# Two chunks' products in four quarters of PSUM's rows, three places for w, test scratch in PSUM, and a planned ScalarE in the first chunks

## Chip, cores and metric

One Trainium2 chip, one core. The metric is the device time of one execution in microseconds (us), smaller is better. Engines: TensorE (PE in the profile, PEld its weight loads), VectorE (DVE), ScalarE (ACT), GpSimd (POOL), and SyncE (SP), whose queue issues nearly all DMAs.

## The reference

A recurrent attention over 4 x 8 heads, 768 positions and head size 40, followed by two feed-forward layers ("MoE") on all 3072 tokens of width 320. Float32 throughout.

```python
state = zeros((B, H, 40, 40))
for t in range(768):
    y[:, :, t] = einsum('bhd,bhde->bhe', r_t, state)
    Sa = einsum('bhde,bhe->bhd', state, a_t)
    state = state * w_t[:, :, None, :] - einsum('bhd,bhe->bhde', Sa, b_t)
    state = state + einsum('bhd,bhe->bhde', v_t, k_t)
x = y as (3072, 320)
x = maximum(maximum(x @ w1, x @ w2), x @ w3) @ w_out        # d_ff 768
h = x @ w_in                                                # d_ff 2048
out = (h * tanh(log1p(exp(h)))) @ w_out2
```

## The kernel before

**Attention.** The 768 positions go in chunks of 32 (C), the 32 heads in two groups of 16, so 48 chunks follow each other, c = 0 to 47. Two chunks make a unit n (24 units). What depends on no state is done ahead of the chain: `pre(n)` takes the running product of w (the scan, L238), its reciprocal by Ln and Exp with a Newton step (L242 to L256), a test of that by Square (L258), scales a (GpSimd, L250), k and b (VectorE, L261 and L265), and multiplies them (L274). Four units make a batch, and `solve(k)` inverts their triangular systems in 31 steps on VectorE (L306, L308). `chain(c)` is the sequence by which chunk c needs the state that chunk c - 1 left: x0 (L382), u (L396), u transposed (L407, L410) and copied beside r (L413), the products of r by u and v (`products`, L349), a triangular mask on them (L418), y and the new state (L430 to L437).

**The products.** `products(h, g)` multiplies r of chunk h by u of chunk h, and r of chunk g = h + 1 by v of chunk g, ahead of time. For each of 16 heads it is a matmul of 40 rows, 32 weight columns and 32 moving columns, which TensorE's records show as two records each. Its output goes to one bank of PSUM, tile `cg`, 128 rows x 512 columns: rows 64 (c % 2) for v, rows 32 further for u, columns 32 ho for head ho. So one call writes two of the four quarters of 32 rows, for u the one half, for v the other.

**Slots.** `run` gives each chunk five slots. In a slot come in turn a step of `chain`, filler (`fill`), a step of the units in `advance`, steps of the solve, and the next step of `chain`. The filler is, in chunks 0 to 5, the conversion of the first MoE's weights (24 blocks), two steps of the pipeline in a slot, a new block every two steps; from chunk LAG = 6 the first MoE's groups of tokens, whose units of 8 matmuls fill TensorE between the steps of the chain, and from chunk 37 on the second MoE's weights beside them.

**The weights' conversion.** The weights come as float64 words. `from64` loads a block (`raw`, 4 places), tests its range (Square, Exp, each with an accumulated sum that the test wants; the element results, written to `t`, are not used), then makes float32 of the two words: ScalarE turns the low word (L580), VectorE shifts and merges the high one into `t` (L581, L582), GpSimd adds (L584). `put` splits it into high and low parts (ScalarE L593, GpSimd L599, VectorE L638).

**w.** `load_w(n)` loads a unit's w to a tile with one place (units 1 to 3 of the start go elsewhere); w is read by the scan and its tile is then scratch up to the Square L258. The load of the next unit's w is traced right behind that Square.

**Order.** The program is built with a planner that places instructions by a model of their times. Inside `tc.manual_schedule(engines=...)` the named engines keep the order of the program: TensorE and VectorE always in attention, ScalarE too. GpSimd and SP take the planner's order. Each engine works off its own queue in order.

## Time and profile before

| | |
|---|---|
| time, median of 3 (lowest to highest) | 1113.77 us (1111.48 to 1116.03) |
| profiled execution: time, span of its instructions | 1112.2 us, 1110.4 us |
| mean granted TensorE clock, share of full speed | 0.99 |
| busy: TensorE, VectorE, ScalarE, GpSimd | 944.8, 864.0, 729.4, 339.0 us |

Times in the rows are us from the start of the span, durations of one instruction are ns where the row says mean. "A <- B" after a row's idle time is what ended that idle time.

### The profile page before, as it was taken

Reading aid. Unit: us, or ns where it says so; the run is one execution under the profiler, and the core shown is the slowest. Engines: PE = TensorE matmul, PEld = TensorE weight load, DVE = VectorE, ACT = ScalarE, POOL = GpSimd, SP = SyncE. Lnnn points to the kernel's source line nnn. Section 1 sums busy time; section 2 is a strip of 40 time slices with the busy share of each in tenths; the row PEclk is TensorE's granted clock in tenths of the full one; section 3 lists DMA queues with packets and bytes.
Section 4 is the critical chain, followed back from the end, with each engine's and each line's share of the span. In section 5 each row is a group of like instructions: output and inputs, shape, how many; then the busy total and the mean of one; then the engine's idle time right before and its main releaser. Section 6 shows DMA issues by size and latency. Waiting matters only on the chain.

```text
span 1110.4 us, 34043 instructions
## 1 busy us (share of the span) xinstructions
PE 944.8 (85%) x14098; PEld 848.1 (76%) x14098; DVE 864.0 (78%) x1650; ACT 729.4 (66%) x1886; POOL 339.0 (31%) x422
## 2 busy tenths in 40 slices
PE   1333435699999999999998999988999999999996
PEld 1222324588888888898897888987899898899896
DVE  7767778968867876876677565879898989888885
ACT  4445775365655665555556777657888787878875
POOL 8436676132322433232113333664020202020000
PEclk9999999999999999999998999998999999999998
DMA  9224442234344343433424443431010101010000
GB/s 244 84 70 118 110 140 49 69 88 110 92 105 106 85 124 75 112 102 79 101 51 120 110 125 106 134 114 43 2 52 1 53 1 53 1 53 1 25 1 27
DMA packets 110614, 87.02 MB, mean 78 GB/s; under 512 B 72740, under 2 KB 89764, under 8 KB 110452
## 3 DMA queue, kind: packets, MB, share of 16 engines
q1 hardware_dynamic: 109712, 84.54, 28.1%
q8 instruction: 113, 1.85, 0.7%
q14 instruction: 49, 0.40, 0.1%
q10 hardware_dynamic: 740, 0.23, 0.1%
HBM read 72.16 MB, written 12.58 MB: 76 GB/s over the span
## 4 chain that ended last, share of the span: by engine, by line
PE 64%; DVE 15%; ACT 10%; issue 3%; DMA 3%; POOL 2%; SPq 0%; ACTq 0%; DVEq 0%; POOLq 0%
PE bps L648 5%; PE cops L976 5%; PE cops L974 5%; PE cops L975 5%; PE cgps L349 4%; PE ys L430 4%; PE bps L798 4%; PE cps L649 4%; PE cps L648 4%; PE cps L650 4%; PE bps L649 4%; PE bps L650 3%; DVE T L308 2%; DVE tv L306 2%; ACT ls L327 2%
## 5 line engine op out<-in xcount | busy, mean ns | idle before, releaser
L648 PE MATMUL bps<-bxh,bw 128*128 128x256 f32 x432 | 139.8, 324 | 9.6 <-ACT mx L755 7.2
L649 PE MATMUL bps<-bxl,bw 128*128 128x256 f32 x432 | 123.8, 287 | 4.2 <-DVE bxl L661 4.2
L650 PE MATMUL bps<-bxh,bw 128*128 128x256 f32 x432 | 122.6, 284 | 0.0
L760 POOL TENSOR_TENSOR hl<-mx,hh 128x256 fp32r<-128x256 f32 x72 | 58.0, 806 | 172.1 <-ACT hh L759 165.1
L648 PEld LDWEIGHTS bps<-bxh,bw 128*128 128x128 f32 x432 | 82.3, 190 | 23.9 <-ACT mx L755 14.5
L250 POOL TENSOR_TENSOR ax<-ax,pp 40x256 f32<-40x256 f32 x96 | 76.7, 817 | 45.6 <-DMA ax<-in_A_dram 16.5
L649 PEld LDWEIGHTS bps<-bxl,bw 128*128 128x128 f32 x432 | 82.9, 192 | 6.7 <-DVE bxl L661 6.5
L308 DVE TENSOR_TENSOR T<-T,tv 128x31 f32<-128x31 f32 (+15 forms) x186 | 81.9, 441 | 6.4
L430 PE MATMUL ys<-rs,ls 128*40 128x72 f32 x1536 | 65.2, 244 | 23.0 <-issue 10.7
L650 PEld LDWEIGHTS bps<-bxh,bw 128*128 128x128 f32 x432 | 82.6, 191 | 0.0
L958 ACT ACTIVATE e<-e 128x512 f32<-128x512 f32 x93 | 58.5, 629 | 34.9 <-DVE e L956 34.4
L286 POOL TENSOR_SCALAR_AFFINE_SELECT ax<-akT 32x256 f32<-32x256 f32 x96 | 48.6, 506 | 107.0 <-DVE akT L281 103.0
L962 DVE SCALAR_TENSOR_TENSOR e<-e,r 128x512 f32<-128x512 f32 x93 | 74.6, 802 | 7.2 <-ACT r L960 7.1
L385 ACT COPY X<-x0ps 128x160 f32<-128x160 f32 x48 | 14.0, 291 | 100.5 <-PE x0ps L382 100.4
L430 PEld LDWEIGHTS ys<-rs,ls 128*40 128x40 f32 x1536 | 56.7, 128 | 29.1 <-issue 12.0
L274 PE MATMUL m<-bk,ax 40*32 40x64 f32 x1536 | 44.2, 261 | 40.7 <-DVE bk L265 21.4
L970 DVE TENSOR_TENSOR gl<-e,gh 128x512 fp32r<-128x512 f32 x93 | 64.6, 695 | 16.3 <-ACT gh L969 15.6
L798 PE MATMUL bps<-hh,bo 128*128 128x256 f32 x360 | 76.2, 294 | 1.3 <-ACT hh L759 1.3
L757 DVE TENSOR_TENSOR mx<-bps,mx 128x256 f32<-128x256 f32 x144 | 60.4, 420 | 20.1 <-PE bps L652 9.8
L418 DVE TENSOR_TENSOR rs<-cgps,cst 64x512 f32<-64x512 f32 x48 | 33.1, 689 | 50.8 <-PE cgps L349 50.4
L274 PEld LDWEIGHTS m<-bk,ax 40*32 40x32 f32 x1536 | 33.6, 132 | 49.0 <-POOL ax L250 29.9
L349 PE MATMUL cgps<-rs,uT 40*32 40x32 f32 x1536 | 64.7, 201 | 7.1 <-ACT uT L410 5.1
(210 smaller groups left out, 3239.6 us busy)
## 6 DMA issues: line engine op xcount, KB each, us to landing
bk<-in_KB_dram SPq DMA_DIRECT2D x24, 448.0 KB
sv<-in_SV_dram SPq DMA_DIRECT2D x96, 80.0 KB
raw<-in_w_dram SPq DMA_DIRECT2D x18, 384.0 KB
w<-in_W_dram SPq DMA_DIRECT2D x21, 231.0 KB
v<-in_VT_dram SPq DMA_DIRECT2D x48, 96.0 KB
rs<-in_RT_dram SPq DMA_DIRECT2D x48, 96.0 KB
cxl<-x SPq DMA_DIRECT2D x12, 384.0 KB
raw<-in_wo_dram SPq DMA_DIRECT2D x13, 320.0 KB
```

Of the source, the lines that this page charges most:

```text
L250: nc.gpsimd.tensor_tensor(out=xv[:, h], in0=xv[:, h], in1=P[ro, h, 0:C], op=ALU.mult)
L274: nc.tensor.matmul(out=ps[32 * zo:32 * zo + 32, cc, jj], lhsT=x[ro, y, 4 * g + jj, cc], rhs=bk[ro, 4 * g + jj, 64 * cc:64 * cc + 64], star ...
L308: nc.vector.tensor_tensor(out=T[:, s + 1:C, 0:s + 1], in0=T[:, s + 1:C, 0:s + 1], in1=tv, op=ALU.subtract)
L349: self.nc.tensor.matmul(out=self.cg[row:row + 32, C * ho:C * ho + C], lhsT=x[0:40, ho], rhs=self.rs[c % 2][0:40, 0:4, ho], start=True, sto ...
L430: nc.tensor.matmul(out=self.ys[64 * y:64 * y + 40, p, 0:72], lhsT=l[:, y, p], rhs=r_[:, :, 4 * (p % 4) + 2 * (1 - y) + p // 4], start=True ...
L648: nc.tensor.matmul(out=ps, lhsT=h[:, k], rhs=xh[:, k], start=(k == 0), stop=False)
L649: nc.tensor.matmul(out=ps, lhsT=h[:, k], rhs=xl[:, k], start=False, stop=False)
L650: nc.tensor.matmul(out=ps, lhsT=l[:, k], rhs=xh[:, k], start=False, stop=False)
L757: after(1, lambda ps=ps, mx=mx: nc.vector.tensor_tensor(out=mx, in0=ps, in1=mx, op=ALU.max))
L798: nc.tensor.matmul(out=pss[d][rows], lhsT=lhsT, rhs=rhs, start=first, stop=last)
L962: nc.vector.scalar_tensor_tensor(out=e, in0=e, scalar=1.0, in1=r, op0=ALU.add, op1=ALU.mult)
L970: nc.vector.tensor_tensor(out=gl, in0=e, in1=gh.bitcast(F32), op=ALU.subtract)
```

## The change

- `products` runs over 8 column places and two halves of the heads: head 8 hi + k of both chunks goes to rows 64 hi (v) and 64 hi + 32 (u), columns 256 (c % 2) + 32 k. One call now writes all four quarters of the rows in turn. The mask is applied in two instructions of 64 x 256 in place of one of 64 x 512.
- w gets a pool of three places, and its load is traced two units ahead, at the head of `pre`.
- In the first MoE's weights the Square and Exp of the range test write to a scratch tile in PSUM (one place), and a block has one more pipeline step between load and test.
- `run` becomes a generator that stops once, before chunk LAG. Up to there ScalarE is not among the engines in program order; from there it is.

```diff
--- before.py
+++ after.py
@@ -162,6 +162,7 @@
         const = pool("a_const", 1)
         pers = pool("a_pers", 1)
         self.p1 = pool("a_1", 1)
+        self.pw = pool("a_w", 3)
         self.ps_m1 = pool("ps_m1", 1, space=PSUM)
         self.ps_kb = pool("ps_kb", 1, space=PSUM)
         self.ps_sm = pool("ps_sm", 1, space=PSUM)
@@ -214,7 +215,7 @@
             t = self.T if n == 2 else self.tr[n // 2]
             self.w[n] = t.rearrange("p t i -> p (t i)")[0:112, 0:528]
         else:
-            self.w[n] = self.p1.tile([128, 528], F32, name="w", tag="w")[0:112]
+            self.w[n] = self.pw.tile([128, 528], F32, name="w", tag="w")[0:112]
         self.nc.sync.dma_start(out=self.w[n], in_=self.A["W"][n // NU, n % NU])
 
     def load_a(self, n):
@@ -232,6 +233,8 @@
 
     def pre(self, n):
         nc, p1 = self.nc, self.p1
+        if NB <= n + 2 < 2 * NU:
+            self.load_w(n + 2)
         x, bk, P = self.ax[n % self.NX], self.bk[n % self.NK], self.pp[n % self.NP][0:R]
         w = self.w.pop(n)
         Pv = P[:, :, 1:33]
@@ -259,8 +262,6 @@
         bv = bk[0:R].rearrange("r p (c s t) -> r (p c) s t", c=2, s=2)
         Qv = Q.unsqueeze(2).to_broadcast([R, 16, 2, C])
         nc.vector.tensor_tensor(out=bv[:, 0:8], in0=bv[:, 0:8], in1=Qv[:, 0:8], op=ALU.mult)
-        if NB - 1 <= n < 2 * NU - 1:
-            self.load_w(n + 1)
         yield
         nc.vector.tensor_tensor(out=bv[:, 8:16], in0=bv[:, 8:16], in1=Qv[:, 8:16], op=ALU.mult)
         if n >= NB:
@@ -342,12 +343,14 @@
 
     def products(self, h, g):
 
-        for ho in range(16):
-            for c, x, row in ((h, self.uT, 32), (g, self.v, 0)):
-                if c is not None:
-                    row += 64 * (c % 2)
-                    self.nc.tensor.matmul(out=self.cg[row:row + 32, C * ho:C * ho + C], lhsT=x[0:40, ho],
-                                          rhs=self.rs[c % 2][0:40, 0:4, ho], start=True, stop=True)
+        for k in range(8):
+            for hi in range(2):
+                for c, x, row in ((h, self.uT, 32), (g, self.v, 0)):
+                    if c is not None:
+                        row += 64 * hi
+                        col = 256 * (c % 2) + C * k
+                        self.nc.tensor.matmul(out=self.cg[row:row + 32, col:col + C], lhsT=x[0:40, 8 * hi + k],
+                                              rhs=self.rs[c % 2][0:40, 0:4, 8 * hi + k], start=True, stop=True)
 
     ZZ = [(jj, zo, 1 - zo // 2, zo % 2) for jj in range(4) for zo in (0, 2, 1, 3)]
 
@@ -415,10 +418,12 @@
         yield
 
         self.products(c, c + 1 if c + 1 < 2 * NCH else None)
-        nc.vector.tensor_tensor(
-            out=r_[64:128, 0:4], in0=self.cg[64 * i:64 * i + 64].rearrange("p (h b i) -> p b h i", b=4, i=8),
-            in1=self.mask[64:128].rearrange("p (b i) -> p b i", b=4).unsqueeze(2).to_broadcast([64, 4, 16, 8]),
-            op=ALU.mult)
+        for hi in range(2):
+            nc.vector.tensor_tensor(
+                out=r_[64:128, 0:4, 8 * hi:8 * hi + 8],
+                in0=self.cg[64 * hi:64 * hi + 64, 256 * i:256 * i + 256].rearrange("p (h b i) -> p b h i", b=4, i=8),
+                in1=self.mask[64:128].rearrange("p (b i) -> p b i", b=4).unsqueeze(2).to_broadcast([64, 4, 8, 8]),
+                op=ALU.mult)
         yield
         yield
 
@@ -515,6 +520,8 @@
         for c in range(NC):
             n, cc = divmod(c, 2)
             chain = self.chain(c)
+            if c == LAG:
+                yield
             for slot in range(5):
                 if slot == 0 and cc == 0 and self.place[n] == 0 and k == self.batch[n]:
                     finish(solve)
@@ -561,18 +568,19 @@
     return stage
 
 
-def from64(nc, stage, src, n, cols, gate, put, beside=False):
+def from64(nc, stage, src, n, cols, gate, put, beside=False, junk=None):
 
     raw, t = stage(n, cols)
     nc.sync.dma_start(out=raw, in_=src.bitcast(I32).rearrange("p k (f w) -> p k f w", w=2))
-    yield
-    yield
+    for _ in range(3 if junk else 2):
+        yield
     low, high = raw[:, :, :, 0], raw[:, :, :, 1]
     tf = t.bitcast(F32)
-
-
-    nc.scalar.activation(out=tf, in_=high.bitcast(F32), func=AF.Square, accum_out=gate.le(2.0 ** 33))
-    nc.scalar.activation(out=tf, in_=tf, func=AF.Exp, scale=-(2.0 ** 20), accum_out=gate.le(0.25))
+    q = junk.tile([128, n, cols], F32, name="junk", tag="junk") if junk else tf
+
+
+    nc.scalar.activation(out=q, in_=high.bitcast(F32), func=AF.Square, accum_out=gate.le(2.0 ** 33))
+    nc.scalar.activation(out=q, in_=q, func=AF.Exp, scale=-(2.0 ** 20), accum_out=gate.le(0.25))
     yield
     if beside:
         nc.vector.tensor_scalar(out=low, in0=low.bitcast(mybir.dt.uint32), scalar1=2.0 ** -29, scalar2=None, op0=ALU.mult)
@@ -628,7 +636,7 @@
         return (x[:, 0:256].rearrange("p (k f) -> p k f", k=2), x[:, 256:512].rearrange("p (k f) -> p k f", k=2),
                 x[:, 512:640])
 
-    def load(self, j, stage, beside=False, pool=False):
+    def load(self, j, stage, beside=False, pool=False, junk=None):
         nc = self.nc
         h, l, m = self.parts(j)
 
@@ -637,7 +645,7 @@
             yield from split_to(nc, h, l, t[:, 0:2], pool)
             nc.vector.tensor_tensor(out=m[64:128], in0=t[64:128, 2], in1=m[64:128].bitcast(F32), op=ALU.subtract)
 
-        return from64(nc, stage, self.src[j], 3, 128, self.gate, put, beside)
+        return from64(nc, stage, self.src[j], 3, 128, self.gate, put, beside, junk)
 
     def mm(self, ps, j, x):
 
@@ -674,6 +682,7 @@
         wp = pool("b_w", 1)
         self.stage = ExitStack()
         self.tmp = staged(pool("b_t", 4, ctx=self.stage))
+        self.junk = pool("b_j", 1, ctx=self.stage, space=PSUM)
         ws = [wp.tile([128, 6, 640], F32R, name="b" + n) for n in ("w1", "w2", "w3")]
         self.w = [Weights(self.nc, A[n], [w[:, j] for j in range(6)], gate) for n, w in zip(("w1", "w2", "w3"), ws)]
 
@@ -695,9 +704,9 @@
     def weights(self):
         for j in range(6):
             for w in self.w:
-                yield w.load(j, self.tmp)
+                yield w.load(j, self.tmp, junk=self.junk)
         for j in range(6):
-            yield from64(self.nc, self.tmp, self.A["wo"][j], 1, DM, self.gate, lambda t, j=j: self.put_out(t[:, 0], j))
+            yield from64(self.nc, self.tmp, self.A["wo"][j], 1, DM, self.gate, lambda t, j=j: self.put_out(t[:, 0], j), junk=self.junk)
 
     def put_out(self, t, j):
         nc, o = self.nc, self.o[:, j]
@@ -831,7 +840,7 @@
         for j, (_, tag, i) in enumerate(low + [(0, "ab0", i) for i in range(3)]):
             self.spots[1, j] = keep, tag, i
         self.raws = [(keep, raw), (keep, "ab0")]
-        self.ts = [(att.p1, "w"), (att.p1, "Q"), (att.const, "rst")]
+        self.ts = [(att.pw, "w"), (att.p1, "Q"), (att.const, "rst")]
         self.loaded, self.running = set(), []
 
     def beside(self, c):
@@ -1203,8 +1212,11 @@
                     if c >= EARLY:
                         moe2.beside(c)
 
+                chunks = att.run(fill)
+                with tc.manual_schedule(engines=IN_ORDER):
+                    next(chunks)
                 with tc.manual_schedule(engines=IN_ORDER | {mybir.EngineType.Activation}):
-                    att.run(fill)
+                    finish(chunks)
                     moe2.jobs = []
                     while moe2.running:
                         moe2.beside(0)
```

## Rows read from the trace of the kernel before

**Rows 1.** The page: the span, the busy time of each engine (its share of the span, instructions), and TensorE's busy share in 40 equal slices, in tenths.

```profile
span 1110.4 us, 34043 instructions
PE 944.8 (85%) x14098; PEld 848.1 (76%) x14098; DVE 864.0 (78%) x1650; ACT 729.4 (66%) x1886; POOL 339.0 (31%) x422
...
PE   1333435699999999999998999988999999999996
```

**Rows 2.** Busy time by stretch: the stretch and its length, then busy us (instructions) of PE, PEld, DVE, ACT and POOL, the granted TensorE clock, the DMA engines' share and GB/s.

```profile
64.00:180.00 116.00, 46.69 (x1134) 38.59 (x1136) 82.08 (x127) 79.00 (x251) 75.56 (x87) 1.00 0.38 106
180.00:216.00 36.00, 21.71 (x534) 18.11 (x529) 33.62 (x72) 14.37 (x45) 13.01 (x18) 1.00 0.31 78
216.00:700.00 484.00, 467.64 (x9850) 423.25 (x9851) 349.94 (x782) 296.26 (x944) 146.85 (x214) 0.99 0.39 99
260.00:280.00 20.00, 19.33 (x396) 17.10 (x395) 18.00 (x37) 11.22 (x37) 6.98 (x10) 1.00 0.37 100
360.00:380.00 20.00, 19.71 (x449) 17.88 (x451) 18.29 (x41) 13.48 (x42) 7.75 (x11) 1.00 0.40 97
```

**Rows 3.** Who waited for whom from 64 to 180 us, by engine and line (SPq: the DMA queue of SP): us in total, how often, the longest.

```profile
DVE t L581 <- ACT t L575: 18.2, 10, 3.5
DVE pp L238 <- DMA w<-in_W_dram: 11.1, 5, 3.5
...
ACT Q L242 <- DVE bk L265: 26.2, 5, 6.4
...
SPq L567 <- POOL t L584: 61.1, 15, 16.9
```

**Rows 4.** The chain of work that ended last, in order of time, from 140 to 217 us: start, us, what.

```profile
143.03 2.73 DMA w<-in_W_dram
...
145.78 1.26 DVE pp L238
...
149.00 1.18 DVE bk L265
...
150.20 0.64 ACT Q L242
...
162.34 2.91 DMA w<-in_W_dram
...
216.71 0.58 PE bps L649
```

**Rows 5.** Timelines of ScalarE and VectorE: start, us, engine, line, operation, out<-in, and in brackets the engine's idle time before it.

```profile
65.76 1.06 ACT L313 ACTIVATE T<-T 128x1024 f32<-128x1024 f32 x1 [13.99 <-DVE tr L312]
...
142.28 0.63 ACT L258 ACTIVATE w<-w 104x512 f32<-104x512 f32 x1
...
150.20 0.63 ACT L242 ACTIVATE Q<-pp 104x512 f32<-104x512 f32 x1 [2.93 <-DVE bk L265]
...
153.90 0.36 DVE L581 TENSOR_SCALAR t<-raw 128x384 int32<-128x384 int32 x1 [2.24 <-ACT t L575]
```

**Rows 6.** Timeline of TensorE: the first two and the last two of the 64 records of one block of products, and the y block after it.

```profile
341.84 0.21 PE L349 MATMUL cgps<-rs,uT 40*32 40x32 f32 x1
341.85 0.21 PE L349 MATMUL cgps<-rs,v 40*32 40x32 f32 x1
...
342.84 0.19 PE L349 MATMUL cgps<-rs,uT 40*32 40x32 f32 x1
342.85 0.19 PE L349 MATMUL cgps<-rs,v 40*32 40x32 f32 x1
...
344.11 1.08 PE L430 MATMUL ys<-rs,ls 128*40 128x72 f32 x28
```

**Rows 7.** Groups of instructions from 216 to 700 us, shapes kept apart: line, engine, operation, out<-in, shapes, count | busy us, mean ns of one | idle time before them.

```profile
L757 DVE TENSOR_TENSOR mx<-bps,mx 128x256 f32<-128x256 f32 x122 | 51.3, 421 | 14.3 <-ACT mx L755 7.3 <-PE bps L652 5.9
L349 PE MATMUL cgps<-rs,uT 40*32 40x32 f32 x1312 | 51.2, 195 | 0.5 <-ACT uT L410 0.4
...
L435 DVE TENSOR_TENSOR sv<-ys,pp 40x320 f32<-40x320 f32 x78 | 37.9, 486 | 31.6 <-PE ys L430 30.8
L418 DVE TENSOR_TENSOR rs<-cgps,cst 64x512 f32<-64x512 f32 x41 | 28.3, 689 | 50.6 <-PE cgps L349 50.4
...
L382 PE MATMUL x0ps<-sv,ax 104*32 104x40 f32 x640 | 19.8, 207 | 0.0
```

**Rows 8.** Timeline of TensorE: two blocks of 32 records that write all four quarters of the rows.

```profile
252.60 0.49 PE L382 MATMUL x0ps<-sv,ax 104*32 104x40 f32 x32
...
254.50 0.67 PE L396 MATMUL ups<-X,tr 32*32 32x40 f32 x32
```

**Rows 9.** Timelines of VectorE and TensorE around two masks, one of the early and one of the late stage.

```profile
98.95 0.69 DVE L418 TENSOR_TENSOR rs<-cgps,cst 64x512 f32<-64x512 f32 x1
...
99.80 2.15 PE L430 MATMUL ys<-rs,ls 128*40 128x72 f32 x32 [4.02 <-DVE rs L418]
...
343.09 0.69 DVE L418 TENSOR_TENSOR rs<-cgps,cst 64x512 f32<-64x512 f32 x1 [1.07 <-PE cgps L349]
...
344.15 0.68 DVE L254 SCALAR_TENSOR_TENSOR w<-pp,Q 104x512 f32<-104x512 f32 x1
```

**Rows 10.** Groups of VectorE's instructions from 64 to 180 us, columns as in rows 7.

```profile
L254 DVE SCALAR_TENSOR_TENSOR w<-pp,Q 104x512 f32<-104x512 f32 x6 | 6.8, 1126 | 0.0
...
L418 DVE TENSOR_TENSOR rs<-cgps,cst 64x512 f32<-64x512 f32 x5 | 3.4, 689 | 0.2
```

## The prediction

> **What bounds the kernel now.** I read the page first, then the stretches, then the waits of the stretch that is not full, then TensorE's blocks in the one that is. The page [rows 1] has TensorE busy for 85% of 1110.4 us, and its slices show where the rest is: the first fifth. The stretches [rows 2] say it in numbers. From 216 to 700 us (chunks 7 to 47, with the first MoE's matmuls as filler) TensorE is busy 467.64 of 484 us: that stage is bound by TensorE, and only shorter TensorE work shortens it. From 64 to 180 us no engine is full: VectorE 82.08 of 116, ScalarE 79.00, GpSimd 75.56, TensorE 46.69. From 180 to 216 VectorE is, 33.62 of 36. The program gives 35 slots (chunks 0 to 6) to the 152 us from 64 to 216, so 4.3 us each.
>
> What holds 64 to 180 up is in the waits [rows 3]. VectorE stands 33.9 us there (116 - 82.08), and two lines hold 29.3 of it: L581, the shift of a weight, waits 18.2 us for ScalarE's Exp on the same tile, and L238, the scan of a unit, 11.1 us for the load of w. ScalarE stands too, 26.2 us at L242 (the unit's Ln) for VectorE's L265. One period shows how they hold each other [rows 4, 5]: only when the Square L258 has ended, at 143.0, is the single w tile free; the load takes 2.73 us, the scan starts at 145.78, L265 follows at 149.0, and ScalarE, in program order, has stood 2.93 us with the next weights' work behind its Ln. From 150.2 it works off that backlog, and now VectorE stands 2.24 us at L581. The next w load starts at 162.34, 19.3 us after the last. Two in-order queues wait for each other in turn; neither is full.
>
> **The change, part by part.**
>
> *Products in four quarters.* A steady block [rows 6] has 64 records; the first starts at 341.84, the last at 342.85, so 1.01 us start to start. They come in pairs, a u and a v 0.01 us apart, a pair every 1.01/32 = 0.032 us: the two quarters of PSUM's rows in use run side by side, and a record waits for the one before it in its own quarter. L382 writes all four quarters, with 32 weight columns as here and 40 moving columns: 32 records in 0.49 us, of which 0.21 is the last one's own length [rows 7, 8], so 0.28/31 = 9.0 ns a record against 1.01/63 = 16.0. If a quarter keeps its 32 ns, four of them give 16 x 0.032 = 0.51 us a block, 0.50 less. At L382's rate it is 63 x 0.009 = 0.57, 0.44 less. I take 0.50, since L382's records have a quarter more columns. From 216 on there are 41 blocks (41 masks, L418; 1312 records of u, 32 each [rows 7]): 41 x 0.50 = 20.5 us, at the other bound 18. The seven blocks before 216 I count at nothing: VectorE comes to them late (it stood 0.2 us before five masks [rows 10]).
>
> The rule that speaks against this part is in the Trainium skill, "TensorE: Matmul & The Clock Gate", section "Wait — 56ns, not 53.3ns?": the distance from start to start never drops below about 25 ns however few the columns are. By it the block would stay where it is and the sum would lose its 20.5. The trace does not agree: 16 ns in L349's blocks, 9 in L382's.
>
> *The mask in two.* L418 takes 0.69 us for 64x512 [rows 7]. Half of it has no row; near ones are 128x256 at 0.42 (L757) and 40x320 at 0.49 (L435) [rows 7], both from PSUM. Two of 0.42 with 0.03 between make 0.87, 0.18 more; two of 0.49 are 0.32 more. I take 0.18, as 256 columns are what is read. VectorE's own time for it is there in the late stage (it stood 1.07 us before this mask [rows 9]); behind it wait VectorE's L757 and TensorE's L430. The mask ends at 343.78 and L430 starts at 344.11, 0.33 us later [rows 6, 9]; the signal between them took 0.16 where TensorE did wait (99.64 to 99.80 [rows 9]). So the cover, one step of the MoE's matmuls, is 0.17: 0.18 just fits, 0.32 would cost 0.15 a chunk or 6 us. In the stretches with VectorE at 18.0 and 18.3 of 20 [rows 2] the solve runs too; there 0.18 us more, in a chunk of 11.8 us (484/41) that gets 0.5 shorter, brings it from 91% to 97%. For both I give back 2 us, between 0 and 6.
>
> *Three places for w, loaded two units ahead.* The load no longer waits for the Square of the unit before, but for one two units older; a period is 19 us and the load 2.7, so it has landed. L238's 11.1 us go. SP gets the load further ahead in a queue in which it stands 61.1 us for raw places anyway [rows 3]; nothing due sooner is behind it.
>
> *Scratch in PSUM, one step later.* Square and Exp no longer write the tile that L581 writes, so L581 waits for the raw load alone: 18.2 us go. The third step leaves time for that load and lengthens a weight's way by half a slot; 24 weights, one a slot, have 30 slots.
>
> *ScalarE planned until chunk 6.* In chunks 0 to 5 ScalarE takes the planner's order in place of the program's. Where L242 is not ready it can take a weight's Square or cast; and before 65.76, where it now stands 13.99 us until the first solve ends [rows 5], those of three weights.
>
> The last three have one answer. 29.3 us of VectorE's stand are removed. Late next are L638, behind ScalarE's cast and GpSimd's add, L254 behind Ln and Exp, L581 behind the raw load, and VectorE itself, which beside GpSimd takes 1.13 us for an L254 that takes 0.68 alone [rows 9, 10]. The upper bound is all of 29.3, less 0.9 for five masks: 28, VectorE then at 83/88 = 94%, as full as in the stretch behind it (93%). At 85% the stretch takes 83/0.85 = 98 and loses 18; at 75% it loses 5. I take 85%, and one more for the 2.4 us it stands from 180 to 216: 19.
>
> **The sum.** Against the profiled execution (1112.2 us, span 1110.4): 1112.2 - 19 - 20.5 + 2 = 1074.7. The median is 1113.77, 1.6 above, so 1076.
>
> **The rivals.**
> (a) *The early stage stays.* Not ScalarE's order but its and GpSimd's work sets the slot, and L638 and L254 take L581's place. For it: 79.00 and 75.56 us in the same 116, each handing to the other. Against: both stand over 35 us. It wins 0 to 8 there: 1112.2 - 4 - 18.5 + 1.6 = 1091. Chance 0.11.
> (b) *The quarters don't run four wide*, by a floor per instruction, as the rule above has it, or by TensorE's order of u and v. For it: L396 writes four quarters too and takes 0.67 us for 32 records, some 15 ns each [rows 8]. Against: L382. Then 1112.2 - 19 + 2 + 1.6 = 1097. Chance 0.08.
> (c) *Slower: ScalarE's planned order is wrong.* It is fixed beforehand by a model's times; where the model lands a raw load earlier than the chip, ScalarE's head stands on it with the chain's copies (L385, L410, L413) behind, and TensorE and VectorE behind those. For it: SP, planned already, stands 61.1 of 116 us. With 18.5 us won later, it decides from 18.5/30 = 0.6 us lost in each slot of chunks 0 to 5; at 1 us a slot, 1112.2 + 30 - 18.5 + 1.6 = 1125. Chance 0.04.
> (d) *More than forecast*: all 29.3 us, and quarters at full rate without the give-back: 1112.2 - 29 - 20.5 + 1.6 = 1064. Chance 0.08.
> The forecast itself, 1069 to 1086 (its terms at 13 to 24 and 15 to 20.5), has 0.66; 0.03 is left for no change at all.
>
> **Range and chances.** 1063 to 1094, from (d)'s value to the far end of (a); it leaves out (b), (c), the left-over and half of (d), 0.19. Within 0.5% (5.6 us), about what a measurement of this kernel can tell from no change, lies only the left-over: faster 0.93, same 0.03, slower 0.04.
>
> **What would show it.** L349's block of 64 records at 0.5 to 0.6 us start to start (at 1.0 it is (b)). No wait of L238 for w, none of L581 for L575. The first MoE matmul, now at 216.71 [rows 4], near 197. From there to the end of attention no more TensorE idle time than now (16.4 us), with L430 waiting for L418 by 0.1 us a time at most. The forecast is wrong if L242, L254 or L638 have new waits of 15 us or more, if ScalarE stands for raw loads, or if the masks make L430 wait in every chunk.

## The result, and the profile after

The changed kernel takes 1088.17 us in the median of four executions (1087.41 to 1090.26), against 1113.9 for the kernel before beside it: ratio 0.9773, interval 0.9748 to 0.9797. That is faster, inside the forecast range and 12 us above the point of 1076. The profiled execution took 1087.56 us. Of all executions below one, of the kernel with one place for w, took 2880 us in place of some 1090 and is left out of its median.

The page's first lines of the kernel after (as [rows 1]):

```profile
span 1085.9 us, 34056 instructions
...
PE 921.8 (85%) x14098; PEld 822.4 (76%) x14098; DVE 876.4 (81%) x1698; ACT 728.8 (67%) x1886; POOL 337.9 (31%) x422
...
PE   1324445799999989999999999898999999999996
```

TensorE lost 23 us of busy time, and its full stretch begins about half a slice earlier. For an account, both executions are cut at the start of three instructions: the first solve's transposition back (L312 before, L313 after), the first MoE matmul, and the last product. The stretch between the first two is called the early stage below, that to the last product the late stage. Stretch and length, then busy us of PE, PEld, DVE, ACT, POOL, clock, DMA share, GB/s; the kernel before:

```profile
64.42:215.72 151.30, 68.12 (x1662) 56.42 (x1663) 115.06 (x196) 93.13 (x295) 88.57 (x104) 1.00 0.36 100
215.72:695.68 479.96, 463.60 (x9793) 419.48 (x9794) 347.20 (x775) 294.67 (x938) 144.86 (x212) 0.99 0.39 98
```

and the kernel after:

```profile
66.50:202.08 135.58, 63.16 (x1663) 50.70 (x1663) 117.25 (x202) 87.03 (x280) 87.69 (x104) 1.00 0.41 111
202.08:670.09 468.01, 445.43 (x9793) 399.76 (x9794) 357.97 (x815) 294.98 (x936) 144.91 (x212) 1.00 0.39 100
```

The account: the start is 2.08 us longer, the early stage 15.72 shorter, the late stage 11.95 shorter, and the rest 1.09 longer (1085.9 - 670.09 against 1110.4 - 695.68). 2.08 - 15.72 - 11.95 + 1.09 = -24.50, and the spans differ by 24.5. In the late stage TensorE's busy time fell by 18.17 us, while the time it stood rose from 16.36 to 22.58, so 6.2 of the 18.2 were given back.

**Early.** VectorE's waits from 64 to 190 us, after, against [rows 3]:

```profile
DVE bw L646 <- ACT bw L601: 11.4, 7, 2.8
DVE rs L422 <- PE cgps L352: 1.6, 1, 1.6
DVE ud L401 <- PE ups L399: 1.0, 1, 1.0
```

Both old lines are gone: no scan waits for w, no shift for the Exp. In their place stands one that the prediction named as late next, the subtraction of a weight behind ScalarE's cast (L638 before, L646 now). The raw loads' queue, 61.1 us in [rows 3], still stands:

```profile
SPq L574 <- POOL t L592: 52.0, 16, 17.8
```

**Late.** A block of products on TensorE, first two and last two records, then the two masks on VectorE and the y block (as [rows 6, 9]):

```profile
326.89 0.21 PE L352 MATMUL cgps<-rs,uT 40*32 40x32 f32 x1
326.90 0.21 PE L352 MATMUL cgps<-rs,v 40*32 40x32 f32 x1
...
327.44 0.19 PE L352 MATMUL cgps<-rs,uT 40*32 40x32 f32 x1
327.46 0.19 PE L352 MATMUL cgps<-rs,v 40*32 40x32 f32 x1
...
327.83 0.88 DVE L422 TENSOR_TENSOR rs<-cgps,cst 64x256 f32<-64x256 f32 x2
...
328.73 1.20 PE L435 MATMUL ys<-rs,ls 128*40 128x72 f32 x32
```

The block takes 0.57 us where it took 1.01, and start to start the 41 blocks of the late stage add up to 26.1 us where they were 44.6 (blocks into which other matmuls fall are longer, in both). The two masks take 0.88 us. What TensorE waited for in the late stage, after:

```profile
PE bps L656 <- ACT mx L764: 8.7, 7, 2.0
PE utps L410 <- DVE ud L401: 5.9, 8, 1.6
PE bps L657 <- DVE bxl L669: 3.0, 10, 0.5
PE ys L435 <- ACT Q L247: 1.0, 3, 0.3
PE bps L807 <- ACT mx L796: 0.7, 1, 0.7
PE x0ps L385 <- PE bps L660: 0.6, 3, 0.2
```

The same before; the last three had no wait there but for 0.2 us at the y block:

```profile
PE bps L648 <- ACT mx L755: 7.2, 6, 2.0
PE utps L407 <- DVE ud L398: 4.1, 4, 1.8
PE bps L649 <- DVE bxl L661: 2.7, 9, 0.4
```

The differences add up to 5.7 of the 6.2 us. In 35 of the 41 chunks the y block starts behind the second mask's end, 0.02 us behind it in the rows above and 0.16 in the median, and no mask makes it wait. In the other six it starts 0.34 to 0.36 us before that end, as its first records need the first mask only; its records then take 1.12 to 1.14 us start to start in place of 0.98. In three of these six it has waited 0.33 us besides. The profile puts this wait (L435) down to ScalarE's L247, but it is for the first mask (shown below, at the half mask). L385's, put down to TensorE itself, is for VectorE too: in its two longest places L440 had ended 0.10 us before.

### The profile page after: what moved, and what is told of

It reads as the page before. It is cut to its first block, busy times and chain, and to the rows that moved or that the text cites. A ratio compares the mean times of both kernels' runs of the same rounds, so it can differ in the third digit from the quotient of the medians.

```text
span 1085.9 us, 34056 instructions
## 1 busy us (share of the span) xinstructions
PE 921.8 (85%) x14098; PEld 822.4 (76%) x14098; DVE 876.4 (81%) x1698; ACT 728.8 (67%) x1886; POOL 337.9 (31%) x422
## 4 chain that ended last, share of the span: by engine, by line
PE 59%; DVE 20%; ACT 10%; DMA 4%; issue 4%; POOL 3%; SPq 0%; ACTq 0%; DVEq 0%; POOLq 0%
PE cops L985 5%; PE cops L983 5%; PE cops L984 5%; PE bps L656 5%; PE cps L656 4%; PE cps L657 4%; PE cps L658 4%; PE ys L435 4%; PE bps L657 3%; DVE T L309 3%; PE bps L658 3%; PE bps L807 3%; DVE tv L307 3%; PE cgps L352 2%; PE cps L659 2%
## 5 line engine op out<-in xcount | busy, mean ns | idle before, releaser
L656 PE MATMUL bps<-bxh,bw 128*128 128x256 f32 x432 | 140.4, 325 | 11.5 <-ACT mx L764 8.7
L657 PE MATMUL bps<-bxl,bw 128*128 128x256 f32 x432 | 124.6, 288 | 4.4 <-DVE bxl L669 4.4
L656 PEld LDWEIGHTS bps<-bxh,bw 128*128 128x128 f32 x432 | 82.8, 192 | 26.4 <-ACT mx L764 16.4
L309 DVE TENSOR_TENSOR T<-T,tv 128x31 f32<-128x31 f32 (+15 forms) x186 | 87.6, 471 | 6.4
L657 PEld LDWEIGHTS bps<-bxl,bw 128*128 128x128 f32 x432 | 83.5, 193 | 6.8 <-DVE bxl L669 6.7
L287 POOL TENSOR_SCALAR_AFFINE_SELECT ax<-akT 32x256 f32<-32x256 f32 x96 | 53.4, 556 | 105.0 <-DVE akT L282 101.0
L435 PE MATMUL ys<-rs,ls 128*40 128x72 f32 x1536 | 65.2, 243 | 19.6 <-DVE rs L422 17.6
L766 DVE TENSOR_TENSOR mx<-bps,mx 128x256 f32<-128x256 f32 x144 | 60.4, 420 | 21.5 <-PE bps L660 11.4
L807 PE MATMUL bps<-hh,bo 128*128 128x256 f32 x360 | 75.2, 290 | 2.0 <-ACT hh L768 1.3
L435 PEld LDWEIGHTS ys<-rs,ls 128*40 128x40 f32 x1536 | 55.9, 126 | 26.6 <-DVE rs L422 18.6
L422 DVE TENSOR_TENSOR rs<-cgps,cst 64x256 f32<-64x256 f32 x96 | 40.6, 423 | 36.7 <-PE cgps L352 34.4
L936 POOL CAST cxh<-cxl 128x1536 fp32r<-128x1536 f32 x5 | 8.7, 1747 | 197.2 <-DMA cxl<-x 197.2
L307 DVE TENSOR_TENSOR tv<-tr,T 128x31 f32<-128x31 f32 (+15 forms) x186 | 67.0, 360 | 2.3
```

The lines of the kernel that those rows point to most:

```text
L307: nc.vector.tensor_tensor(out=tv, in0=abT[:, s, s + 1:C].unsqueeze(2).to_broadcast([128, n, s + 1]), in1=T[:, s, 0:s + 1].unsqueeze(1).to_ ...
L309: nc.vector.tensor_tensor(out=T[:, s + 1:C, 0:s + 1], in0=T[:, s + 1:C, 0:s + 1], in1=tv, op=ALU.subtract)
L435: nc.tensor.matmul(out=self.ys[64 * y:64 * y + 40, p, 0:72], lhsT=l[:, y, p], rhs=r_[:, :, 4 * (p % 4) + 2 * (1 - y) + p // 4], start=True ...
L656: nc.tensor.matmul(out=ps, lhsT=h[:, k], rhs=xh[:, k], start=(k == 0), stop=False)
L657: nc.tensor.matmul(out=ps, lhsT=h[:, k], rhs=xl[:, k], start=False, stop=False)
L766: after(1, lambda ps=ps, mx=mx: nc.vector.tensor_tensor(out=mx, in0=ps, in1=mx, op=ALU.max))
```

## The experiments

The profiled executions, cut as above (us; "first solve starts" is the first solve's first transposition, some 27 us ahead of the first cut; "stands" is TensorE's idle time in the late stage). Times and ratios stand with each experiment.

| kernel | first solve starts | early stage | late stage | stands |
|---|---|---|---|---|
| before | 37.69 | 151.30 | 479.96 | 16.4 |
| after | 39.76 | 135.58 | 468.01 | 22.6 |
| products alone | 39.24 | 151.50 | 469.01 | 21.0 |
| all but the products | 40.12 | 136.15 | 481.13 | 17.1 |
| scratch and third step alone | 37.17 | 149.55 | 476.72 | 16.9 |
| after, one place for w | 39.56 | 136.43 | 466.55 | 21.9 |
| after, ScalarE in program order | 38.82 | 138.32 | 470.63 | 21.8 |
| products and w alone | 39.10 | 142.20 | 465.86 | 22.3 |
| after, no scratch, two steps | 39.93 | 129.13 | 466.27 | 22.1 |
| after, scratch, two steps | 39.56 | 129.31 | 469.74 | 22.0 |
| after, subtraction a step later | 39.27 | 129.82 | 467.97 | 21.8 |
| after, second mask left out | 40.48 | 134.13 | 464.87 | 18.5 |
| after, half the columns | 39.81 | 135.72 | 467.38 | 21.6 |
| no scratch, two steps, start held | 37.71 | 129.22 | 465.63 | 20.8 |

### Which part wins where

The kernel before with the new `products` and the two masks alone:

```diff
+        for k in range(8):
+            for hi in range(2):
...
+        for hi in range(2):
+            nc.vector.tensor_tensor(
```

> The kernel before with the products in four quarters and the two masks alone; all else as before. Theory (two independent parts, as the sum has them): the late stage alone gets shorter. Blocks of products 0.56 us start to start in place of 1.01, 41 of them, 18.5 us less TensorE work; TensorE's idle time in the late stage rises from 15.9 to about 22 us, because the stretches with a solve are now bound by VectorE; so 11 to 12 us in all, 1102. The early stage stays within 2 us. Rival (the idle time was brought by the other parts, which reach the late stage through w's places or through a different order): idle time stays near 16 and the run gains 17 to 18, 1096.

Measured: 1102.11 us, ratio 0.9885 (0.986 to 0.9911). That was the theory's case: the early stage does not move, the late one loses 11 us, and TensorE stands 4.6 us more in it. Most of the give-back thus belongs to the products and their masks.

The kernel after with the old `products` and one mask:

```diff
-        for k in range(8):
-            for hi in range(2):
...
+        for ho in range(16):
```

> The changed kernel with the products and the mask of before: three places for w, scratch in PSUM with a later test, and the planned ScalarE. Theory: the early stage gains what it gains in the changed kernel, 13 to 14 us to the first matmul of the MoE (of which the start loses 2), the late stage nothing: 1100, TensorE's idle time in the late stage 16. Rival (the early gain came in part from the faster blocks of products, which run at half rate there): the early stage gains only 9 to 11, 1103 to 1105.

Measured: 1100.41 us, ratio 0.9877 (0.985 to 0.9903). The mirror image: the early stage moves alone, 136.15. In the late stage TensorE stands 0.7 us more than before. The two savings, 11.3 and 13.0 us against the 1113.37 measured beside them, add up to 24.2 of the change's 25.7.

### The parts of the early stage

Scratch and third step alone, on the kernel before:

```diff
+        self.junk = pool("b_j", 1, ctx=self.stage, space=PSUM)
...
-    yield
-    yield
+    for _ in range(3 if junk else 2):
+        yield
```

> The kernel before with the scratch in PSUM and the later test alone. Theory: the stage of weights falls from 151.3 to 139 to 143 us, 1102 to 1105 in all, VectorE still waits some 8 to 11 us for the load of w. Rival (any two do it, one alone does not, since the scan's wait then takes the place of the test's): the stage stays at 146 or more, 1109 or more.

Measured: 1109.2 us, ratio 0.9986 (0.9965 to 1.0006): no difference that can be measured, the rival's case. VectorE's and ScalarE's waits from 64 to 190 us say why:

```profile
DVE pp L238 <- DMA w<-in_W_dram: 16.6, 5, 4.2
DVE bw L639 <- ACT bw L594: 6.8, 5, 2.0
DVE akT L281 <- ACT ab L279: 5.5, 4, 1.9
...
ACT Q L242 <- DVE bk L265: 30.2, 5, 8.0
```

The shift's 18.2 us are gone. The scan's wait has grown from 11.1 to 16.6, that for ScalarE's copies (L281) from 1.5 to 5.5, and ScalarE, in program order, still stands at L242, 30.2 us: one link cut leaves the circle closed through the others. The 6.8 us at L639 are new and another thing, the price of the third step (next section). The scratch alone, with two steps, was not run, so 1.75 us is what the two give together.

The kernel after with one place for w, loaded behind the Square:

```diff
-            self.w[n] = self.pw.tile([128, 528], F32, name="w", tag="w")[0:112]
+            self.w[n] = self.p1.tile([128, 528], F32, name="w", tag="w")[0:112]
...
-            self.load_w(n + 2)
...
+            self.load_w(n + 1)
```

> The changed kernel with one place for w, loaded as before. Theory: the scan waits for the load of w again, 1.7 to 3.5 us in each of five units, 11 us of VectorE's time, of which 6 to 11 reach the end: 1094 to 1099. Rival (with ScalarE planned the Square comes early enough that the load is in time): within 2 us of the changed kernel.

Measured: 1090.24 us in the median of three executions, ratio 0.9799 (0.9767 to 0.983): the rival's case, or very near it. The scan waits for w again, but only 2.3 us, and the stage is 0.9 longer.

The kernel after with ScalarE in program order throughout:

```diff
-                with tc.manual_schedule(engines=IN_ORDER):
+                with tc.manual_schedule(engines=IN_ORDER | {mybir.EngineType.Activation}):
```

> The changed kernel with ScalarE in program order throughout. Theory (the planned order is what keeps VectorE fed, but delays the start): the start is 1 to 2 us earlier than in the changed kernel, the stage behind it 5 to 10 us longer, with VectorE or ScalarE standing at L242's successor for L265 again; in all 1092 to 1096. Rival (w's places and the scratch alone removed the waits; the planned order only cost the start): 1086, faster than the changed kernel by 2.

Measured: 1087.52 us, ratio 0.9753 (0.9722 to 0.9784), no different from the change as a whole, and nearer to the rival. The stage is 2.7 us longer where the theory had 5 to 10: VectorE waits 5.8 us at L282 for ScalarE's copies, and L646 waits 11.8, as in the kernel after.

Both of these still had the other two parts. The last of the group has the products and the three places for w alone:

```diff
-                yield w.load(j, self.tmp, junk=self.junk)
+                yield w.load(j, self.tmp)
...
-                with tc.manual_schedule(engines=IN_ORDER):
+                with tc.manual_schedule(engines=IN_ORDER | {mybir.EngineType.Activation}):
```

> The kernel after without scratch and third step and with ScalarE in program order throughout: the products and the three places for w alone. It asks whether one broken link of the circle between ScalarE and VectorE is enough when that link is w's. Theory (any two of the three parts are needed, as scratch alone won only 1.75 us): the shift of a weight on VectorE waits 10 us or more for ScalarE's Exp, early stage 140 to 148 us, time 1092 to 1100. Rival (the early load of w is enough by itself): early stage 129 to 134, time 1080 to 1086.

Measured: 1091.74 us, ratio 0.981 (0.9781 to 0.9838); early stage 142.20. The theory's case: with w early, the wait for the Exp is back and the only large one.

```profile
DVE t L589 <- ACT t L583: 15.8, 9, 3.5
...
ACT Q L245 <- DVE bk L266: 17.0, 5, 5.3
```

So the early load of w by itself is worth 9 us of the stage, scratch and third step by themselves 1.75, and with any two of the three parts the stage is at 129 to 138; the two pairs at 136 and 138 have the third step. Planned order by itself was not tried.

### The third step

The kernel after without scratch, and so with two pipeline steps:

```diff
-                yield w.load(j, self.tmp, junk=self.junk)
+                yield w.load(j, self.tmp)
```

> The changed kernel without the scratch in PSUM and without the later test: Square and Exp write the tile that VectorE's L581 writes, two steps after the load. Without the planned ScalarE (e3_act_in_order) the stage of weights took 138.3 us, without w's places (e4_one_w) 136.4, with all three 135.6, before 151.3. Theory (the scratch carries most of the 15.7, and of the other two each is covered by the rest): the stage is 143 to 149 us, 1096 to 1101 in all, and VectorE waits for ScalarE's test by 8 us or more. Rival (any two of the three do nearly all, since each breaks the circle of the two queues): the stage is 137 to 140, 1088 to 1092.

Measured: 1081.8 us, ratio 0.9724 (0.9707 to 0.9742), faster than the change itself: taking a part out wins 6.4 us by the medians (5.4 by the ratios, as the kernel before beside it was 1.0 us faster). Theory and rival both missed it, as both had the stage longer without the scratch; the rival, that two of the three parts do nearly all, was the nearer. L646 waits 1.1 us in place of 11.4. Either the scratch itself or the third step costs, so the scratch was kept and only the step taken back:

```diff
-    for _ in range(3 if junk else 2):
+    for _ in range(2):
```

> The kernel after with the scratch tile, but two pipeline steps between load and test as before, in place of three. It parts the scratch from the added step. Theory (the third step is what costs: it brings ScalarE's and GpSimd's casts and VectorE's subtraction L646 into one slot): L646 waits under 3 us for ScalarE's cast, the early stage falls from 135.6 to 129 to 131 us, time 1080 to 1084, as without scratch. Rival (the scratch itself costs, by its one place or by the PSUM writes): early stage 134 to 137, time 1086 to 1090.

Measured: 1084.2 us (1078.45 to 1085.15), ratio 0.973 (0.9689 to 0.977), early stage 129.31. VectorE's waits from 64 to 190 us, all of them:

```profile
DVE w L257 <- ACT Q L247: 1.8, 3, 1.4
DVE ud L401 <- PE ups L399: 0.9, 1, 0.9
DVE bw L646 <- ACT bw L601: 0.3, 1, 0.3
```

It is the step. A slot makes two pipeline steps and a new block starts every two, so the parity of a block's step decides which of its operations share a slot. The subtraction L646 comes one step after the cast L601. With two steps between load and test the cast is the last operation of a slot and the subtraction belongs to the next; with three, both fall in one slot, and so do the shift and GpSimd's add behind it. In the kernel after, the timeline shows GpSimd's add, the cast behind it and VectorE standing for both:

```profile
105.81 1.96 POOL L592 TENSOR_TENSOR t<-t,raw 128x384 int32<-128x384 int32 x2
106.84 0.60 ACT L601 CAST bw<-t 128x128 fp32r<-128x128 f32 x2 [1.17 <-POOL t L592]
107.17 0.75 DVE L646 TENSOR_TENSOR bw<-t,bw 64x128 fp32r<-64x128 f32 x1 [2.63 <-ACT bw L601]
```

If that is so, three steps do no harm once the subtraction too comes one step later:

```diff
             yield from split_to(nc, h, l, t[:, 0:2], pool)
+            if junk:
+                yield
```

> The changed kernel with VectorE's subtraction of the third weight column block (L646 there) one pipeline step later. In the changed kernel VectorE stands 11.4 us at it, in 7 places, for ScalarE's cast, and is busy 117.6 of 136 us. Theory (what is left to win there is that wait): it goes, the stage falls by 5 to 10 us to 126 to 131, 1079 to 1083 in all. Rival (VectorE's order moves the wait on: the next one in the order, L589 or the scan's L257, stands for the same backlog of ScalarE and GpSimd): the stage stays within 3 us, 1085 to 1089.

Measured: 1081.43 us, ratio 0.9714 (0.9695 to 0.9734), early stage 129.82, and the subtraction waits 1.3 us. Three kernels without the shared slot, with and without scratch, agree at 129 to 130 us.

### What the late stage gave back

The second of the two masks left out from chunk 2 on, so that half of the masked products are old ones; it takes 17 us of VectorE's work out and nothing of TensorE's:

```diff
-        for hi in range(2):
+        for hi in range(2 if c < 2 else 1):
             nc.vector.tensor_tensor(
```

> The changed kernel with the second of the two mask instructions left out from chunk 2 on, so that half of each chunk's masked products are old ones. It takes 0.42 us a chunk from VectorE, 17 us in the late stage, against the 7 us that the split added. Theory (the 6 us of new TensorE idle time in the late stage come from VectorE being full in the stretches of the solve): the idle time falls from 22.6 to 14 to 18 us and the new waits at the y block, at x0 and at u transposed go; the late stage takes 460 to 464 in place of 468. Rival (the shorter TensorE work itself uncovers the chain's latencies, whatever VectorE has to do): idle time stays at 21 to 23, the late stage at 467 to 469.

Measured in one execution: 1083.75 us; late stage 464.87, TensorE stands 18.5 us in it, both just outside the theory's ranges and far from the rival's. The waits sit where a solve runs on VectorE beside the chain. Timelines of VectorE, ScalarE and TensorE in one such place, the kernel after:

```profile
256.89 0.78 DVE L309 TENSOR_TENSOR T<-T,tv 128x240 f32<-128x240 f32 x1
257.70 0.88 DVE L422 TENSOR_TENSOR rs<-cgps,cst 64x256 f32<-64x256 f32 x2
...
257.80 0.18 ACT L247 ACTIVATION_READ_ACCUMULATOR Q<-Q 104x1 f32 x1
...
258.22 1.36 PE L435 MATMUL ys<-rs,ls 128*40 128x72 f32 x32 [0.33 <-ACT Q L247]
...
266.34 0.44 PE L410 MATMUL utps<-cst,ud 128*128 128x128 f32 x2 [0.77 <-DVE ud L401]
```

and with half the mask:

```profile
257.23 0.42 DVE L422 TENSOR_TENSOR rs<-cgps,cst 64x256 f32<-64x256 f32 x1
...
257.31 0.19 ACT L247 ACTIVATION_READ_ACCUMULATOR Q<-Q 104x1 f32 x1
...
257.75 1.20 PE L435 MATMUL ys<-rs,ls 128*40 128x72 f32 x32 [0.32 <-ACT Q L247]
...
264.99 0.44 PE L410 MATMUL utps<-cst,ud 128*128 128x128 f32 x2 [0.29 <-DVE ud L401]
```

With VectorE lighter than before the change (338.3 us busy in the late stage against 347.2), 4 of the 6 us are gone: L410, behind VectorE's queue, recovers (3.6 us in place of 5.9; 4.1 before), and L385's wait goes. L435 keeps its 1.0 us. Its wait ends 0.10 us behind the first mask (257.70 + 0.42 above, 257.23 + 0.42 here) and 0.24 to 0.25 behind L247, in all three places of both kernels, and in the trace TensorE's wait for VectorE's semaphore ends 0.05 us behind that mask. So it is the first mask that the y block waits for, and that mask stands behind a step of the solve (L309); leaving out the second cannot shorten it. L656 for ScalarE's mx stays too, 8.6 us against 7.2 before: shorter matmuls that cover less of the same work on ScalarE fit that, but this share is argued, not isolated.

### What a record of the block costs

From chunk 2 on half of the moving columns, so that half of every product is not computed:

```diff
-                        self.nc.tensor.matmul(out=self.cg[row:row + 32, col:col + C], lhsT=x[0:40, 8 * hi + k],
-                                              rhs=self.rs[c % 2][0:40, 0:4, 8 * hi + k], start=True, stop=True)
+                        self.nc.tensor.matmul(out=self.cg[row:row + 32, col:col + (C if c < 2 else C // 2)], lhsT=x[0:40, 8 * hi + k],
+                                              rhs=self.rs[c % 2][0:40, 0:4 if c < 2 else 2, 8 * hi + k], start=True, stop=True)
```

> The kernel after, but from chunk 2 on each matmul of the products moves 16 columns in place of 32, so half of every product is left out. It asks what a record of the block costs: its columns or a fixed share of time. Theory (columns set the rate in a quarter, 32 ns for 32 columns): the block of 64 records falls from 0.56 us start to start to 0.3 to 0.4, and the late stage (468.0 us from the first MoE matmul to the last product) gets 4 to 9 us shorter, time 1079 to 1084. Rival (a floor of about 8 to 9 ns from record to record over all quarters, whatever the columns): the block stays at 0.53 to 0.57, late stage 466 to 469, time 1086 to 1090.

Measured in one execution: 1088.71 us, late stage 467.38. One block, its first two and last two records:

```profile
326.64 0.20 PE L352 MATMUL cgps<-rs,uT 40*32 40x16 f32 x1
326.64 0.20 PE L352 MATMUL cgps<-rs,v 40*32 40x16 f32 x1
...
327.17 0.18 PE L352 MATMUL cgps<-rs,uT 40*32 40x16 f32 x1
327.19 0.18 PE L352 MATMUL cgps<-rs,v 40*32 40x16 f32 x1
```

Undisturbed blocks take 0.551 us start to start, against 0.564 with all columns. The rival holds as far as columns go: 8.7 to 9.0 ns from record to record, with 16 as with 32. That this is a floor over all quarters is not shown: within its own quarter a record follows the last by some 35 ns here and by 32 ns in the two quarters of before, so it may as well be one for each quarter.

### The start

The kernel after without scratch and third step, the weights' ScalarE work of the first two slots held behind the start's last copy of ab, and the load of w for unit 5 moved behind those of v:

```diff
-                    for _ in range(2):
-                        next(weights, None)
+                    with tc.issue_after(att.held) if c == 0 and slot < 2 else ExitStack():
+                        for _ in range(2):
+                            next(weights, None)
```

> The kernel after without scratch and third step, and with the start put in order: the weights' work of ScalarE in the first two slots may not be placed ahead of the start's last copy of ab, and the load of w for unit 5 comes behind the loads of v. Theory (the first solve starts late, at 39.8 to 39.9 us in place of 37.7, because planned weights' tests stand on ScalarE ahead of the copies): first solve's transposition at 37.2 to 38.5 us, early stage 129 to 131, time 1078.5 to 1081. Rival (the start varies from execution to execution, whatever ScalarE's order): start at 38.8 to 40.5 and time within 1 us of 1081.8.

Measured: 1078.42 us (1075.27 to 1084.0), ratio 0.97 (0.9655 to 0.9745), the lowest median of all. Its first solve starts at 37.71, as in the kernel before. VectorE's last two waits ahead of it, the kernel after and then this one:

```profile
34.65 0.45 DVE L282 STREAM_TRANSPOSE akT<-m 128x256 f32<-128x256 f32 x1 [3.16 <-ACT ab L280]
...
39.39 0.45 DVE L282 STREAM_TRANSPOSE akT<-m 128x256 f32<-128x256 f32 x1 [3.71 <-ACT ab L280]
```

```profile
33.83 0.45 DVE L282 STREAM_TRANSPOSE akT<-m 128x256 f32<-128x256 f32 x1 [2.33 <-ACT ab L280]
...
37.33 0.45 DVE L282 STREAM_TRANSPOSE akT<-m 128x256 f32<-128x256 f32 x1 [2.48 <-ACT ab L280]
```

In the kernel after, the Squares and Exps of four weights stand on ScalarE ahead of the copies. The two waits are 0.83 and 1.23 us shorter here, and their sum is the whole difference of the starts, 39.76 - 37.71. But the start varies without planned work too: with products alone, ScalarE in program order and one w, it was 39.24, the scan having waited 2.6 us for a load of w. In the table the eight kernels with a planned, unheld ScalarE start at 39.27 to 40.48, the five in program order at 37.17 to 39.24, 1.4 us apart in the mean. So where the 2 us of this one start lie is shown, and that a planned ScalarE starts later fits all of the table; holding the weights and moving the load of w were not tried apart. And the time's interval overlaps that of the kernel without scratch: a gain in the median over 1081.8 is not shown.

## Why the prediction was right, and where its steps were not

**Products in quarters: right, at the low bound.** Forecast 20.5 us with 18 as the other bound; TensorE's busy time fell by 18.2. The choice between the two ends failed: I argued that L382's records are longer by a quarter of their columns, so 32 columns would go at 8 ns. Half the columns changed nothing, so columns (16 or 32) are not what spaces these records, and L382's 9.0 ns [rows 7, 8] was the row to take; why L396's records stand 15 ns apart stays open. Rival (b) is out: u and v do run four wide, and a block is not kept at 1.0 us. By the rule of the Trainium skill, "TensorE: Matmul & The Clock Gate", section "Wait — 56ns, not 53.3ns?", 64 starts would need 1.6 us, an estimate from its 25 ns. The trace does not agree, with 0.56.

**The masks: right in size, and not in the cover everywhere.** A half takes 0.42 us (mean 423 ns), as the row of L757 gave [rows 7]. In 35 of the 41 chunks the cover fits. In the other six, all behind a step of the solve, the masks do hold the y block, by the 0.33 us of three waits and the 0.15 to 0.16 us by which its records are drawn out: 1.9 us in all. The sign "by 0.1 us a time at most" did not hold there.

**The give-back: mis-sized.** Forecast 2 us of a possible 6; measured 6.2, and so the sign "no more TensorE idle time than now" failed as well. The mechanism was in the main the named one, the stretches in which the solve fills VectorE: of the 5.7 us of new waits 3.5 are for VectorE (L410, L435, L385, L657), and with half a mask 4 us return. What I left out is that shorter TensorE work also uncovers waits that VectorE has no part in (L656 and L807 for mx, 2.2 us more).

**The early stage: 19 forecast, 15.7 measured, and a step of it wrong.** That the two waits go and that VectorE then stands at 85% fitted (117.25/135.58 = 86%). But the 85% was a middle between bounds, and what held it there was no property of VectorE: without the shared slot it reaches 121.50/129.31 = 94%, my upper bound, and the stage loses 22 us (some 3 of VectorE's 121.50 us are the same instructions taking longer, see the last section). The wrong step is the sentence that the third pipeline step "lengthens a weight's way by half a slot" and nothing else. Half a slot moves every later operation of a block into the other half, and that cost 6.3 us. I named L638 behind the cast as late next and gave it no price but the sign of 15 us or more, which its 11.4 us stay under.

**What was not in the sum.** The start, 2.1 us longer in this execution, and the tail, 1.1. With the measured terms in their places, 1112.2 + 2.1 - 15.7 - 18.2 + 6.2 + 1.1 = 1087.7. Rival (c), the planned order gone wrong, shows only here: at the start planned tests did stand ahead of needed copies, for about 2 us, and not in every slot.

**The range, and some luck in it.** All the misses lie on one side, 3.3 us in the early stage, 2.3 in the products, 4.2 in the give-back and 3.2 in start and tail. The 1088.17 lies above the 1069 to 1086 that the forecast's own terms allowed, and inside the range only because that reached up to rival (a), an early stage that stays (to 1094; by (a)'s own terms its far end is 1095). That stage did not stay.

## What to carry to other kernels

When two engines' queues wait for each other in turn, cutting one link may buy little (scratch with the third step: 1.75 us; w: 9) and the second most of the rest, so test the parts in pairs and not only one by one. When a software pipeline gets a step more, work out for every later operation in which slot it now falls and with whom; a step that adds no work cost 6 us here, and one more step gave it back. When a stage is bound by one engine, what is taken off that engine comes back only as far as its other waits were not hiding under it: 12 of 18 us here.

## What the runs showed of the hardware that was not expected

- In the late stage, small matmuls (40 rows, 32 weight columns) that write four quarters of PSUM's rows in turn start 8.7 to 9.0 ns apart with 32 columns as with 16; written to two quarters, they start 16 ns apart [rows 6]. It is no rule for every block that writes four quarters: L396's records stand some 15 ns apart [rows 8].
- VectorE's instructions can take much longer while GpSimd works. Without the shared slot (scratch, two steps) VectorE is busy 121.50 us of the early stage's 129.31, in the kernel after 117.25 of 135.58, with one instruction of 0.96 us more. GpSimd is busy as long in both (87.49 and 87.69), but the two are busy at the same time for 85.8 us in place of 78.0. The shift of a weight grew most, the kernel after and then the other:

```profile
L589 DVE TENSOR_SCALAR t<-raw 128x384 int32<-128x384 int32 x18 | 7.6, 425 | 0.1
L589 DVE TENSOR_SCALAR t<-raw 128x384 int32<-128x384 int32 x18 | 12.3, 686 | 0.5
```

  In the kernel before, the same shift (L581) took 0.36 us in the 12 places where GpSimd stood, and 0.72 to 0.88 in the five with GpSimd busy beside it for three quarters of it or more. Not every overlap costs: in the kernel after, six that GpSimd works beside throughout take 0.33 to 0.36.
- The granted clock of the early stage did not matter to it. With products alone it was 0.81 of the full 2.4 GHz on average (row below), in the kernel before 1.00, and the stage took 151.50 and 151.30 us; without scratch it was 0.79, with scratch and two steps 1.00, and the stage took 129.13 and 129.31. Nor did TensorE's records get longer: a block of products takes 0.95 us start to start in products alone at 173 us, where the clock is at 0.50 (1.2 GHz), and 0.94 in the early stage of the kernel after at 1.00. In the late stage, at 1.00 too, it takes 0.56.

```profile
65.96:217.46 151.50, 62.29 (x1662) 50.64 (x1663) 115.99 (x203) 93.16 (x295) 86.45 (x104) 0.81 0.35 100
```
